# First batch of a fused attention and two MLPs: tile arithmetic and conversion steps set tile by tile

## The chip, the core and the metric

The kernel runs on one core of a Trainium2 chip. The metric is device time in microseconds (us). The engines are named as the profile names them: PE (TensorE, matmuls), DVE (VectorE), ACT (ScalarE), POOL (GpSimd) and SP (SyncE, which here only issues DMAs). Each engine runs its own instructions in order; so does each queue of DMA issues.

## The reference

```python
def _attn_ref(q, k, v, p):                       # batch 8, heads 8, seq 576, head_dim 64; p: 32 rows
    p_packed = sm_attn(p, k, v)
    return sm_attn(q, p_packed, p_packed)
def _moe_ref(x, w_in, w_out):                    # 4608 tokens, 512 -> 2048 -> 512
    h = x @ w_in
    g = h - np.tanh(h)
    return g @ w_out
def _moe2_ref(x, w_in, w_out, s, b):
    h = x @ w_in
    r = np.maximum(h, 0.0)
    return (s * (r * r) + b) @ w_out
```

The second MLP takes what the first returns, and the first takes the attention's output with the heads side by side. The weights of both MLPs come as 64-bit floats.

## The kernel before

Every product of the MLPs is made of three fp32r products of high and low parts: a value is rounded to fp32r (high), and the difference is the low part. The weights are first converted from 64-bit words to fp32 (`to_f32`, lines 113 to 130: one pass on ACT, line 119, then four on DVE, lines 121, 123, 126 and 129), and then, for the second layer, split (`split_seq`: the high part by ACT, line 138, the low part by DVE or POOL, line 140). First-layer weights come in four blocks of 512 columns, each converted in two halves of 1024 columns per partition (`w1_steps`); second-layer weights in 16 blocks of 512 (`wo1_steps`, blocks 0 to 15).

The tokens are worked on in 8 batches, each in two halves of 288 tokens. A tile is one block of 128 hidden units for one half: `mm1` (six matmuls, line 464), the tile arithmetic h - tanh(h) with its high and low parts, and, two or three tiles later, `mm2` (twelve matmuls, line 504). The first-layer weights are folded with the packed values of the batch (`make_z`), so that a tile needs z of its batch and the attention weights a2h and a2l of its half. A batch has 32 tiles; in the first batch they run as four parts of 8: first half with hidden blocks 0 to 7, second half with 0 to 7, first half with 8 to 15, second half with 8 to 15. Partial sums of the first two parts go to memory and come back (lines 522 and 527).

The tile arithmetic has three forms. "v": tanh on ACT, the subtraction on DVE (line 473), high part on ACT, low part on DVE (line 135). "b": the subtraction on DVE within the PSUM bank (line 481), high part by ACT, then PE subtracts the high part in the bank (line 487) and ACT copies the low part out (line 488). "p": as "b", but PE also subtracts the tanh (line 484), and DVE does nothing.

All other work is in two generators, from which steps are drawn: `fill` (conversion of the first MLP's weights, then the attention of the next batch: key scores `stage1`, z, `second_stage`) and `more` (conversion of the second MLP's weights, into memory). Six slots lie in each tile, one within mm1, one behind it, four within mm2. In the first batch, until second-layer block 15 is converted, each slot draws from `fill` by `SLOTS` (5, 3, 4 or 1 steps per six slots, by part) and each mm1 by `AFTER`; then, until the first half of batch 1 is through its attention, each mm1 draws four more. Within `first_weights` groups of generators run in turn, and the next group's first steps are drawn `AHEAD` of its turn. `until` draws steps by force where a tile needs what isn't done.

`FIRST_W` says at which steps of batch 0's own attention, before any tile, the first ten conversion steps (block 0 of the first layer) are drawn. The k, v and q of batches 1 to 7 are loaded through POOL's queue (lines 170, 177, 178 and 240), in pieces of 128 bytes for k and q; weights, partial sums and p through SP's.

## Time and profile before

| | us |
|---|---|
| median of 3 runs (1517.79 to 1522.28) | 1519.46 |
| the profiled execution | 1515.79 |
| its span | 1514.0 |
| PE busy | 1463.3 (97%) |
| DVE busy | 1074.3 (71%) |
| ACT busy | 754.1 (50%) |
| POOL busy | 357.9 (24%) |

The shares are means over a span of very different stages. The first batch is the first ninth of it, and it is there that PE's busy tenths fall below nine. So the page gives only the frame, and the rows further down are read from the trace within the first 172 us. Busy times of PE are modelled, since matmuls are pipelined: a busy share of PE in a short stretch is an upper end.

### The profile page before, as it was taken

The numbers are of one execution on the slowest core, as the hardware profiler recorded it, in microseconds if no ns is written. First come the engines' busy times: TensorE is split into PE (matmuls) and PEld (weight loads), VectorE is DVE, ScalarE is ACT, GpSimd is POOL, SyncE is SP. The second block draws the span as 40 slices with busy tenths as digits, with TensorE's granted clock in tenths as the row PEclk, the third lists the DMA queues.
The fourth block names the chain that finished last, engine by engine and source line by source line (L and its number), as shares of the span: only waits on it lengthen the run. The fifth ranks groups of instructions, "written<-read, shape, count | busy, mean of one in ns | idle before, by whom it ended". The sixth has DMA issues, their size and how long they took to land.

```text
span 1514.0 us, 28111 instructions
## 1 busy us (share of the span) xinstructions
PE 1463.3 (97%) x10508; PEld 1377.0 (91%) x10508; DVE 1074.3 (71%) x2058; ACT 754.1 (50%) x1459; POOL 357.9 (24%) x576
## 2 busy tenths in 40 slices
PE   6779899999999999999999999999999999999998
PEld 4668798998988889889999999999999999999998
DVE  5886878879687887875555767767777775565564
ACT  4554344444444344443344556656667655454443
POOL 0248452634447274543001000000021000000000
PEclk7899999999999999999999999999999999999999
DMA  9446355544535354332428466465487987676683
GB/s 283 162 135 169 105 147 138 155 132 120 150 98 151 92 141 118 103 94 95 147 100 308 178 229 235 172 260 214 194 296 284 312 258 199 217 239 200 216 248 84
DMA packets 252185, 271.62 MB, mean 179 GB/s; under 512 B 112784, under 2 KB 191888, under 8 KB 252048
## 3 DMA queue, kind: packets, MB, share of 16 engines
q1 hardware_dynamic: 225952, 222.68, 44.9%
q0 software_dynamic: 22368, 46.17, 11.4%
q8 instruction: 82, 1.34, 0.4%
q10 hardware_dynamic: 3728, 0.98, 0.3%
q14 instruction: 55, 0.45, 0.1%
HBM read 161.61 MB, written 108.13 MB: 178 GB/s over the span
## 4 chain that ended last, share of the span: by engine, by line
PE 79%; issue 7%; DVE 6%; DMA 3%; POOL 3%; ACT 2%; SPq 1%; DVEq 0%; POOLq 0%; ACTq 0%
PE acc L504 22%; PE h L464 11%; PE Y L1271 9%; PE Y L1045 8%; PE Z L1271 6%; PE X L1045 6%; PE Z L1045 6%; PE X L1271 6%; PE zp L367 2%; POOL k L170 1%; DMA k<-in_k_dram 1%; DVE gl L135 1%; PE pv L339 1%; SPq L194 1%; DMA g<-g 1%
## 5 line engine op out<-in xcount | busy, mean ns | idle before, releaser
L504 PE MATMUL acc<-gh,wo 128*128 128x288 f32 x2040 | 418.6, 296 | 0.2 <-DVE wo L140 0.2
L504 PEld LDWEIGHTS acc<-gh,wo 128*128 128x128 f32 x2040 | 329.8, 189 | 0.5 <-DVE wo L140 0.4
L504 PE MATMUL acc<-gl,wo 128*128 128x288 f32 x1020 | 309.8, 304 | 5.7 <-ACT wo L138 2.8
L472 ACT ACTIVATE t<-h 128x288 f32<-128x288 f32 x240 | 98.8, 412 | 304.4 <-PE h L464 263.5
L504 PEld LDWEIGHTS acc<-gl,wo 128*128 128x128 f32 x1020 | 192.4, 189 | 34.7 <-issue 20.0
L464 PE MATMUL h<-a2h,z 128*128 128x288 f32 x1024 | 213.9, 297 | 1.5 <-ACT z L445 1.5
L473 DVE TENSOR_TENSOR t<-h,t 128x288 f32<-128x288 f32 x240 | 107.5, 448 | 139.5 <-ACT t L472 138.8
L944 DVE TENSOR_TENSOR x<-B,x 128x768 fp32r<-128x768 f32 x158 | 147.0, 950 | 74.3 <-ACT x L1201 60.4
L464 PE MATMUL h<-a2l,z 128*128 128x288 f32 x512 | 157.9, 308 | 9.8 <-ACT gl L488 6.4
L464 PEld LDWEIGHTS h<-a2h,z 128*128 128x128 f32 x1024 | 165.0, 189 | 2.2 <-ACT z L445 1.7
L240 POOL DMA_DIRECT2D q<-in_q_dram x224 | 135.3, 612 | 130.7 <-DVE qT L374 109.3
L1045 PE MATMUL Y<-x,w 128*128 128x384 f32 x864 | 158.5, 336 | 0.0
L1271 PE MATMUL Y<-x,w 128*128 128x384 f32 x864 | 153.4, 335 | 0.0
L1045 PEld LDWEIGHTS Y<-x,w 128*128 128x128 f32 x864 | 151.3, 188 | 0.0
L1271 PEld LDWEIGHTS Y<-x,w 128*128 128x128 f32 x864 | 150.2, 188 | 0.5 <-ACT x L1201 0.3
L170 POOL DMA_DIRECT2D k<-in_k_dram x224 | 136.6, 617 | 50.2 <-DVE kT L290 40.7
L464 PEld LDWEIGHTS h<-a2l,z 128*128 128x128 f32 x512 | 97.4, 190 | 27.1 <-ACT gl L488 9.4
L1201 ACT CAST x<-B 128x768 fp32r<-128x768 f32 x116 | 93.8, 834 | 42.6 <-DMA B<-g 30.2
L135 DVE TENSOR_TENSOR gl<-t,gh 128x288 fp32r<-128x288 f32 x239 | 110.8, 463 | 0.0
L1045 PE MATMUL X<-x,w 128*128 128x384 f32 x576 | 108.1, 336 | 0.0
L1045 PE MATMUL Z<-x,w 128*128 128x384 f32 x576 | 107.9, 336 | 0.0
L1271 PE MATMUL X<-x,w 128*128 128x384 f32 x576 | 103.0, 336 | 1.5 <-DVE w L944 1.5
(181 smaller groups left out, 2236.4 us busy)
## 6 DMA issues: line engine op xcount, KB each, us to landing
g<-g SPq DMA_DIRECT2D x190, 384.0 KB, 3.3
B<-g SPq DMA_DIRECT2D x116, 384.0 KB, 4.7
w<-w_d POOLq DMA_DIRECT2D x28, 512.0 KB, 6.1
B<-x2t SPq DMA_DIRECT2D x24, 384.0 KB, 5.4
g<-s SPq DMA_DIRECT2D x23, 384.0 KB, 2.8
out_dram<-g SPq DMA_DIRECT2D x184, 48.0 KB, 1.9
x2t<-xs SPq DMA_DIRECT2D x15, 576.0 KB, 3.7
w1s<-in_moe_w_in_dram SPq DMA_DIRECT2D x16, 512.0 KB, 8.1
```

The costliest lines, as they stand in the source:

```text
L135: (eng or nc.vector).tensor_tensor(out=lo, in0=x, in1=hi.bitcast(F32), op=ALU.subtract)
L170: nc.gpsimd.dma_start(out=t[p0:p0 + 32, e], in_=rows[a][:, e, :, u * 32:u * 32 + 32])
L240: nc.gpsimd.dma_start(out=t[p0:p0 + 32], in_=src.rearrange("(n r) d -> r n d", r=32))
L367: nc.tensor.matmul(ps[e][i * M:(i + 1) * M, :rhs(i).shape[-1]], pblk[b][r, h // 4, h % 4 * M:h % 4 * M + M], rhs(i)[r], start=True, stop=True)
L464: nc.tensor.matmul(h[:, :HB], zt[:, zi, g, f0:f0 + P], a[:, g], start=(n == 0), stop=(n == 3 * G - 1))
L472: nc.scalar.activation(t, h[:, :HB], AF.Tanh)
L473: nc.vector.tensor_tensor(out=t, in0=h[:, :HB], in1=t, op=ALU.subtract)
L504: nc.tensor.matmul(acc[m][:, :HB], w[:, m * P:(m + 1) * P], x, start=(j == js[0] and i == 0), stop=(j == js[-1] and i == 2))
L944: self.nc.vector.tensor_tensor(out=o, in0=a, in1=b, op=op)
L1045: self.nc.tensor.matmul(bank[:, f, :self.TH], w[:, f, a, kt], x[:, b, kt], start=(p in ("P1", "P5", "P6") and m == 0), stop=(m == 5), skip ...
L1201: self.nc.scalar.copy(self.xs[(7 * self.NBK + n) % self.XS][:, 0], self.ready[0])
L1271: nc.tensor.matmul(bank[:, ft, :T], w[:, kk, u, ft], x[:, v, kk], start=first and p in ("P1", "P5", "P6"), stop=last, skip_group_check=True)
```

## The change

It sets, for the first batch, the form of the arithmetic of each of the 32 tiles (`HOW`: now 16 "p", 9 "b" and 7 "v") and the number of steps drawn in each tile's six slots (`STEPS`; these replace `SLOTS`, `AFTER` and `CATCH_UP`). It gives the low parts of blocks 2 to 11 to DVE, which POOL made. It issues the loads of batch 1's k, v and q on SP's queue instead of POOL's, and draws them ahead of the conversion of first-layer block 3 instead of behind it. Only conversions are drawn ahead of their turn, one step each. The first steps of the two halves of first-layer block 0 are drawn at steps 10 and 29 of the attention instead of 23 and 40, with the others moved too. `minus`, the negated identity, is made by POOL from zeros instead of by ACT.

```diff
-    AFTER, SLOTS = (6, 5, 4, 1), (5, 3, 4, 1)
-    HOW = "p" * 8, "b" * 8, "v" * 8, "v" * 8
-    AHEAD, CATCH_UP, FIRST_W = 13, 4, (23, 24, 25, 26, 27, 40, 41, 42, 43, 44)
+    STEPS = 9, 13, 14, 11, 15, 10, 12, 15, 0, 6, 9, 13, 7, 5, 0, 2, 6, 3, 10, 5, 6, 10, 11, 11, 18, 14, 15, 13, 12, 13, 10, 8
+    HOW = "ppbbpppppppppbvvvvvpppvvbbbpbbbp"
+    FIRST = (0, 0, 8), (1, 0, 8), (0, 8, 16), (1, 8, 16)
+    FIRST_W = 10, 15, 17, 25, 27, 29, 32, 40, 43, 44
...
-                        nc.gpsimd.dma_start(out=t[p0:p0 + 32, e], in_=rows[a][:, e, :, u * 32:u * 32 + 32])
+                        (nc.gpsimd if b > 1 else nc.sync).dma_start(out=t[p0:p0 + 32, e], in_=rows[a][:, e, :, u * 32:u * 32 + 32])
...
-            yield from split_wo(j, "wo1", nc.gpsimd if 1 < j < 12 else nc.vector, x)
+            yield from split_wo(j, "wo1", nc.vector, x)
...
-                    if i == min(AHEAD, 4 * len(group)) and n + 1 < len(groups):
-                        for g in groups[n + 1]:
-                            next(g)
+                    if i == len(group) and n + 1 < len(groups):
+                        for f, g in groups[n + 1]:
+                            if f in (w1_steps, wo1_steps):
+                                next(g)
...
-        nc.scalar.mul(minus, ident, -1.0)
+        nc.vector.memset(csum, 0.0)
+        nc.gpsimd.tensor_tensor(out=minus, in0=csum[:, 0], in1=ident, op=ALU.subtract)
...
+                [(second_loads,)],
                 [(w1_steps, 3, 0)], [(w1_steps, 3, 1)],
-                [(wo1_steps, 12), (wo1_steps, 13), (second_loads,)],
-                [(first_z, 3), (wo1_steps, 14), (wo1_steps, 15)])
+                [(first_z, 3), (wo1_steps, 12), (wo1_steps, 13)],
+                [(wo1_steps, 14), (wo1_steps, 15)])
...
-            if ("wo", NF - 1) not in done:
-                n = SLOTS[part[0]]
-                for _ in range(ticks[0] * n // 6 - (ticks[0] - 1) * n // 6):
+            if ("wo", NF - 1) in done and ticks[0] % 3 == 1:
+                next(more, None)
+            if ("a", 1, 0) in done or tile[0] >= len(STEPS):
+                next(fill, None)
+                return
+            n = STEPS[tile[0]]
+            for _ in range(ticks[0] * n // 6 - (ticks[0] - 1) * n // 6):
+                if ("a", 1, 0) not in done:
                     next(fill)
-                return
-            if ticks[0] % 3 == 1:
-                next(more, None)
-            next(fill, None)
...
-                    if ("wo", NF - 1) not in done:
-                        for _ in range(AFTER[part[0]]):
-                            next(fill)
-                    elif ("a", 1, 0) not in done:
-                        for _ in range(CATCH_UP):
-                            next(fill)
```

The order of instructions at three places, before and after. The changed file is three lines longer or shorter at places, so that line 121 of before is line 122 of after, and so on.

First place: DVE around the end of the conversion of second-layer blocks 10 and 11 (`t_10`, `t_11`, `wo1s_10`, `wo1s_11`; `wo1_10` and `wo1_11` hold the split blocks; `h_0_1_5` and `t_0_1_6` belong to tiles 13 and 14; `w1_3` is first-layer block 3). Before:

```order
L126 SCALAR_TENSOR_TENSOR t_10_933<-wo1s_10_761,t_10_933 128x512
L126 SCALAR_TENSOR_TENSOR t_11_935<-wo1s_11_763,t_11_935 128x512
L481 TENSOR_TENSOR h_0_1_3_964<-h_0_1_3_964,t_0_1_3_976 128x288
L129 SCALAR_TENSOR_TENSOR wo1s_10_761<-wo1s_10_761,t_10_933 128x512
L129 SCALAR_TENSOR_TENSOR wo1s_11_763<-wo1s_11_763,t_11_935 128x512
L481 TENSOR_TENSOR h_0_1_4_998<-h_0_1_4_998,t_0_1_4_1013 128x288
L121 TENSOR_SCALAR w1_3_836<-w1_3_836 128x1024
```

After:

```order
L130 SCALAR_TENSOR_TENSOR wo1s_10_758<-wo1s_10_758,t_10_920 128x512
L130 SCALAR_TENSOR_TENSOR wo1s_11_760<-wo1s_11_760,t_11_922 128x512
L141 TENSOR_TENSOR wo1_10_1010<-wo1s_10_758,wo1_10_1010 128x512
L141 TENSOR_TENSOR wo1_11_1012<-wo1s_11_760,wo1_11_1012 128x512
L482 TENSOR_TENSOR h_0_1_5_1034<-h_0_1_5_1034,t_0_1_5_1043 128x288
L474 TENSOR_TENSOR t_0_1_6_1093<-h_0_1_6_1086,t_0_1_6_1093 128x288
L474 TENSOR_TENSOR t_0_1_7_1117<-h_0_1_7_1110,t_0_1_7_1117 128x288
L136 TENSOR_TENSOR gl_1_0_1_7_1121<-t_0_1_6_1093,gh_1_0_1_7_1120 128x288
L122 TENSOR_SCALAR w1_3_862<-w1_3_862 128x1024
```

The two low parts now stand on DVE, and between them and block 3 only the arithmetic of tiles 13 to 15.

Second place: SP's queue from the load of second-layer block 13 (`wo1s`, 128x512) to that of blocks 14 and 15 (`wo1s`, 128x2x512); `x2t` and `xp` are partial sums. Before:

```order
L522 DMA x2t<-xs_0_906 512x1x288
L599 DMA wo1s_1033<-in_moe_w_out_dram 128x512
L229 DMA pc_1085<-in_p_dram 128x2x64 x2
L581 DMA wo1s_1088<-in_moe_w_out_dram 128x2x512
L522 DMA x2t<-xs_1_1273 512x1x288
```

After:

```order
L600 DMA wo1s_1038<-in_moe_w_out_dram 128x512
L230 DMA pc_1061<-in_p_dram 128x2x64 x2
L171 DMA k_0_0_1067<-in_k_dram 32x9x32 x8
L171 DMA k_0_1_1076<-in_k_dram 32x9x32 x8
L178 DMA v_0_1125<-in_v_dram 64x4x320
L179 DMA v_0_1125<-in_v_dram 64x4x256
L241 DMA q_0_0_0_1137<-in_q_dram 32x9x32 x4
L241 DMA q_0_0_1_1142<-in_q_dram 32x9x32 x4
L241 DMA q_0_1_0_1147<-in_q_dram 32x9x32 x4
L241 DMA q_0_1_1_1152<-in_q_dram 32x9x32 x4
L582 DMA wo1s_1229<-in_moe_w_out_dram 128x2x512
```

Thirty-four loads of batch 1 now stand ahead of blocks 14 and 15.

Third place: ACT around its first pass over second-layer block 14 (`t_14`); `t_0_0_8` is the tanh of tile 16, `t_0_0_10` that of tile 18, `t_0_0_11` that of tile 19. Before:

```order
L138 CAST wo1_13_1179<-wo1s_13_1033 128x512
L488 CAST gl_0_1_6_1112<-h_0_1_6_1072 128x288
L119 ACTIVATE t_14_1200<-wo1s_7_1088 128x512
L485 CAST gh_0_1_7_1167<-h_0_1_7_1135 128x288
L119 ACTIVATE t_15_1217<-wo1s_7_1088 128x512
L432 CAST z_0_3_1189<-zp_0_3_0_1190 128x512
L472 ACTIVATE t_0_0_8_1220<-h_0_0_8_1208 128x288
```

After:

```order
L473 ACTIVATE t_0_0_10_1259<-h_0_0_10_1250 128x288
L135 CAST gh_1_0_0_10_1262<-t_0_0_9_1204 128x288
L120 ACTIVATE t_14_1266<-wo1s_7_1229 128x512
L433 CAST z_0_3_1231<-zp_0_3_0_1232 128x512
L433 CAST z_0_3_1231<-zp_0_3_1_1233 128x512
L480 ACTIVATE t_0_0_11_1295<-h_0_0_11_1287 128x288
L136 CAST gh_1_0_0_11_1299<-t_0_0_10_1259 128x288
```

The pass stands two to three tiles later, right behind tile 18's tanh and ahead of tile 19's.

## Rows read from the trace of the kernel before

**Rows 1.** Busy time by stretch: stretch, length, PE, PEld, DVE, ACT, POOL, clock, DMA.

```profile
36.00:94.90 58.90, 46.79 (x284) 37.14 (x284) 52.03 (x91) 34.67 (x74) 10.76 (x8) 0.89 0.45 164
94.90:171.60 76.70, 65.65 (x578) 52.64 (x576) 57.54 (x132) 36.25 (x96) 55.85 (x88) 1.00 0.58 143
...
111.40:171.60 60.20, 54.78 (x497) 44.01 (x497) 42.97 (x110) 26.84 (x75) 42.51 (x71) 1.00 0.59 145
171.60:262.00 90.40, 88.56 (x794) 80.21 (x788) 73.78 (x194) 43.04 (x114) 41.28 (x68) 1.00 0.49 130
```

**Rows 2.** PE's timeline: start, duration; the first matmuls of tiles 16 and 32.

```profile
111.38 0.40 PE L464 MATMUL h<-a2l,z 128*128 128x288 f32 x1 [1.49 <-ACT gl L488]
...
171.62 0.40 PE L464 MATMUL h<-a2l,z 128*128 128x288 f32 x1
```

**Rows 3.** DVE's groups by line and shape, 14 to 260 us: busy us, mean ns | idle.

```profile
L473 DVE TENSOR_TENSOR t<-h,t 128x288 f32<-128x288 f32 x48 | 21.5, 448 | 25.3 <-ACT t L472 25.2
L135 DVE TENSOR_TENSOR gl<-t,gh 128x288 fp32r<-128x288 f32 x47 | 21.0, 446 | 0.0
L126 DVE SCALAR_TENSOR_TENSOR t<-wo1s,t 128x512 int32<-128x512 int32 x15 | 10.9, 754 | 0.0
...
L123 DVE TENSOR_SCALAR t<-t 128x512 int32<-128x512 int32 x16 | 8.0, 536 | 0.0
L121 DVE TENSOR_SCALAR t<-t 128x512 f32<-128x512 f32 x16 | 7.5, 498 | 2.7 <-ACT t L119 2.5
...
L126 DVE SCALAR_TENSOR_TENSOR cv<-w2s,cv 128x512 int32<-128x512 int32 x6 | 4.1, 684 | 0.1
...
L481 DVE TENSOR_TENSOR h<-h,t 128x288 f32<-128x288 f32 x8 | 3.7, 458 | 3.1 <-ACT t L479 3.1
...
L140 DVE TENSOR_TENSOR wo<-wo1s,wo 128x512 fp32r<-128x512 f32 x5 | 3.2, 682 | 0.1
...
L123 DVE TENSOR_SCALAR cv<-cv 128x512 int32<-128x512 int32 x6 | 2.5, 419 | 0.0
L121 DVE TENSOR_SCALAR cv<-cv 128x512 f32<-128x512 f32 x6 | 2.5, 413 | 0.0
```

**Rows 4.** DVE's timeline: start, duration, instruction, idle time before it.

```profile
27.18 0.85 DVE L389 STREAM_TRANSPOSE t<-s 128x288 f32<-128x288 f32 x2 [0.29 <-PE s L367]
...
93.63 1.28 DVE L129 SCALAR_TENSOR_TENSOR wo1s<-wo1s,t 128x512 int32<-128x512 int32 x2
...
97.73 1.69 DVE L123 TENSOR_SCALAR w<-w 128x1024 int32<-128x1024 int32 x1
...
102.94 0.69 DVE L123 TENSOR_SCALAR w<-w 128x1024 int32<-128x1024 int32 x1
...
136.25 1.10 DVE L290 STREAM_TRANSPOSE kT<-k 128x288 f32<-128x288 f32 x2 [1.35 <-DMA k<-in_k_dram]
...
166.79 0.83 DVE L418 TENSOR_TENSOR a2l<-a,a2h 128x288 fp32r<-128x288 f32 x2 [0.95 <-ACT a2h L416]
```

**Rows 5.** POOL's timeline, its last low parts and its first loads of batch 1.

```profile
95.82 3.04 POOL L140 TENSOR_TENSOR wo<-wo1s,wo 128x512 fp32r<-128x512 f32 x2 [4.97 <-ACT wo L138]
98.81 6.77 POOL L170 DMA_DIRECT2D k<-in_k_dram  x10
```

**Rows 6.** PE's timeline in a "p" tile: the subtraction of the tanh, and the next matmul.

```profile
66.54 0.65 PE L484 MATMUL h<-t,minus 128*128 128x288 f32 x2
66.81 0.51 PE L464 MATMUL h<-a2l,z 128*128 128x288 f32 x1
```

**Rows 7.** ACT's groups by line and shape, 36 to 172 us.

```profile
L488 ACT CAST gl<-h 128x288 fp32r<-128x288 f32 x16 | 6.4, 398 | 3.7 <-PE h L487 3.7
```

**Rows 8.** SP's timeline: DMA issues, with their count.

```profile
99.28 0.94 SPq L229 DMA_DIRECT2D pc<-in_p_dram  x2
...
1429.28 3.92 SPq L1233 DMA_DIRECT2D out_dram<-g  x8
```

**Rows 9.** DMA issues, 98 to 140 us: count, size, median us to landing.

```profile
wo1s<-in_moe_w_out_dram SPq DMA_DIRECT2D x1, 1024.0 KB, 8.3
```

More of the change, by code (lines that the diff above doesn't have):

```diff
@@ L176, in load_v @@
         src = v[b, 4 * g:4 * g + 4].rearrange("h (r c) d -> r h (c d)", c=C)
-        nc.gpsimd.dma_start(out=t[:R], in_=src[:, :, :CT * D])
-        nc.gpsimd.dma_start(out=t[R:, :, :(C - CT) * D], in_=src[:, :, CT * D:])
+        (nc.gpsimd if b > 1 else nc.sync).dma_start(out=t[:R], in_=src[:, :, :CT * D])
+        (nc.gpsimd if b > 1 else nc.sync).dma_start(out=t[R:, :, :(C - CT) * D], in_=src[:, :, CT * D:])
         v_t[b, g] = t.rearrange("r h (c d) -> r h c d", c=CT)
@@ L239, in load_q @@
                         p0 = (2 * e + u) * 32
-                        nc.gpsimd.dma_start(out=t[p0:p0 + 32], in_=src.rearrange("(n r) d -> r n d", r=32))
+                        (nc.gpsimd if b > 1 else nc.sync).dma_start(out=t[p0:p0 + 32], in_=src.rearrange("(n r) d -> r n d", r=32))
                 q_t[b, hf, g, hp] = t
@@ L639, in in_turn @@
         def in_turn(*groups):
-            groups = [[call_late(g) for g in group] for group in groups]
+            groups = [[(f, f(*a)) for f, *a in group] for group in groups]
             for n, group in enumerate(groups):
-                for i, _ in enumerate(both(group)):
+                for i, _ in enumerate(both([g for _, g in group])):
                     yield
-                    if i == min(AHEAD, 4 * len(group)) and n + 1 < len(groups):
-                        for g in groups[n + 1]:
-                            next(g)
-        def call_late(f):
-            g, *a = f
-            yield from g(*a)
+                    if i == len(group) and n + 1 < len(groups):
+                        for f, g in groups[n + 1]:
+                            if f in (w1_steps, wo1_steps):
+                                next(g)
         def until(key, gen):
@@ L814, in slot @@
                 next(fill, None)
-            if ("wo", NF - 1) not in done:
-                n = SLOTS[part[0]]
-                for _ in range(ticks[0] * n // 6 - (ticks[0] - 1) * n // 6):
+            if ("wo", NF - 1) in done and ticks[0] % 3 == 1:
[6 more added lines that the diff above has]
+                if ("a", 1, 0) not in done:
                     next(fill)
-                return
-            if ticks[0] % 3 == 1:
-                next(more, None)
-            next(fill, None)
+        tile = [-1]
         owed = [0]
@@ L834, in pack_attention_two_mlps @@
             else:
-                parts = [(hf, js) for js in (range(NF // 2), range(NF // 2, NF)) for hf in range(2)]
+                parts = [(hf, range(j0, j1)) for hf, j0, j1 in FIRST]
             for hf, js in parts:
@@ L848, in pack_attention_two_mlps @@
                     c = j // CH
+                    tile[0] += 1
                     until(("z", b, c), fill)
@@ L851, in pack_attention_two_mlps @@
                     h = mm1(b, hf, j, slot)
-                    if ("wo", NF - 1) not in done:
-                        for _ in range(AFTER[part[0]]):
-                            next(fill)
-                    elif ("a", 1, 0) not in done:
-                        for _ in range(CATCH_UP):
-                            next(fill)
                     if j % CH == CH - 1:
                         mm1_done.add((b, hf, c))
-                    how = HOW[part[0]][j - js[0]] if b == 0 else "v"
+                    how = HOW[tile[0]] if b == 0 else "v"
                     on_pe = how != "v"
```

## The prediction

> **What bounds the kernel now.** I read the table by stretches first. From 171.6 us on, the second batch takes 90.4 us for its 32 tiles with TensorE (PE) busy for 88.56 us: PE is the bound there, and 90.4 / 32 = 2.83 us is what a tile costs with all that belongs to it [rows 1]. The first batch is another matter: its 32 tiles need 36.0 to 171.6 us, 135.6 us, and PE waits. Tile numbers below count from 0 in program order; tile 32, the first of the second batch, starts at 171.62 us [rows 2]. Nothing in the diff touches what comes after it, so the whole effect is the shift of that one moment.
>
> Inside the first batch I split at 94.9 us, where VectorE (DVE) ends the last conversion step of second-layer block 11 (93.63 + 1.28) [rows 4]. Before that point DVE is busy for 52.03 of 58.9 us, 88%: it is the bound. After it DVE has 57.54 in 76.7 us, 75%, and nothing is full [rows 1]. So before 94.9 us the change is priced by DVE's work; behind it by how closely DVE and PE can be packed.
>
> **The change, part by part.** *Tile arithmetic (HOW).* Before: 8 tiles "p" (nothing on DVE), 8 "b" (one subtraction), 16 "v" (two). After: 16, 9, 7. A "v" costs DVE 21.5/48 + 21.0/47 = 0.895 us, a "b" 3.7/8 = 0.46 us [rows 3]. Before 16 x 0.895 + 8 x 0.46 = 18.0, after 7 x 0.895 + 9 x 0.46 = 10.4: -7.6 us. Of this -0.9 lies ahead of 94.9 us (two "b" more in tiles 2 and 3, four "b" fewer in tiles 8 to 11) and -6.7 behind it. PE and ScalarE (ACT) take it over: 8 passes with the fp32 tanh, after each of which the next matmul starts 0.27 us later [rows 6], and 9 more subtractions of gh, taken at the same 0.27 as an upper end: 4.6 us on PE; 9 x 0.40 = 3.6 us on ACT [rows 7]. Both have that much idle time in this batch.
>
> *Low parts of blocks 2 to 11 on DVE instead of POOL.* 10 x 3.2/5 = +6.4 us of DVE [rows 3]. Against it: while POOL runs such a subtraction, DVE instructions stretch. The step at 97.73 us took 1.69 us beside POOL's pair at 95.82, the same step at 102.94 us 0.69 [rows 4, 5]. Over all, the 512-wide steps of the first batch against the same steps on the second MLP's weights, which have no such neighbour: 16 x (0.498 - 0.413) + 16 x (0.536 - 0.419) + 15 x (0.754 - 0.684) = 4.3 us [rows 3], and with the 1.0 us of the one wide step 5.3. That the stretch goes away with POOL's work is the better reading of these rows; the other end is 0. I take -5.3, all but 1.0 of it ahead of 94.9 us. Also, block 11 was ready only when POOL ended, 95.82 + 3.04 = 98.86 us [rows 5].
>
> *Steps by tile (STEPS), no catching up.* The same conversions, emitted elsewhere: behind block 11's split stand only four tile subtractions until tile 16, and the eight wide steps of first-layer block 3 follow that tile instead of preceding it (order, first place). Five steps on the second MLP's weights stand before tile 32 where nine stood. The four that go, three of 128 columns and one of 896, are an estimate of 1280 x 0.684/512 = 1.7 us [rows 3], moved into the second batch, where PE is the bound and DVE has 90.4 - 73.8 = 16.6 us idle [rows 1]: free. If that cover were gone they would cost their 1.7 us.
>
> *Loads of batch 1 by SP.* POOL issues ten in 6.77 us [rows 5]; for SP the nearest row is a store in pieces of 128 bytes, eight in 3.92 us, 0.49 us each [rows 8]. POOL's time is off the path. But SP's queue runs in order, and now 16 + 2 + 16 of these loads stand between the load of block 13 and that of blocks 14 and 15 (order, second place). This is the one place where the change adds a wait; it is the first rival. The last k transposes waited 1.35 us for their load [rows 4]. The Trainium skill, "SBUF — State Buffer", in its box on the "DVE blocks DMA" trap, says that a DVE instruction in a two-port mode keeps POOL from writing its descriptors, and that issuing from SP avoids it; by that rule the 1.35 us would go, and the sum below would read 1.35 us less. The trace shows POOL's ten loads without a gap, so I take 0.
>
> *Two conversions begun sooner in the attention.* DVE reaches the score transposes at 27.18 us having waited 0.29 us for PE [rows 4]: the conversions are not what holds it, and starting them sooner gains nothing. Ends: a gain of 0.3, and a loss if ACT's two wide passes, which now stand among the exponentials, come too early; at 0.398 us for 288 columns [rows 7] a 1024-wide pass is an estimate of 1.4 us, so at most 2.8. Taken: 0. Building "minus" on POOL: 0, it is read long after.
>
> **The sum.** Block 11 ready: 94.9 + 6.4 - 0.9 - 4.3 = 96.1 us. Three tiles with next to nothing on DVE (tile 13 to 16) at 2.83: tile 16 starts at 104.6. DVE work left to tile 32: 57.5 - 6.7 - 1.0 - 1.7 - 1.8 (the four subtractions) = 46.3 us. At what share? Before, from tile 16 at 111.4 us on it was 43.0 of 60.2, 71%, in the second batch 73.8 of 90.4, 82% [rows 1, 2]. Both limits are near each other here: 16 tiles x 2.83 = 45 us on PE and some 4 us of new subtractions. I take the middle, 76%: 60.9 us. Tile 32 starts at 165.5, which is 6.1 us sooner. The ends: 82% gives 161.1 (-10.5), 71% gives 169.8 (-1.8). The profiled execution took 1515.79 us (span 1514.0), so it would be 1509.7; the median of the runs shown is 1519.46, 3.7 above it, and the same shift puts the median at 1513.4.
>
> **Rivals.** *1. SP's queue gives the gain back.* Block 13's load can go when block 11 is done, 96.1; then 0.94 for p, as before, and 34 x 0.49 = 16.7 [rows 8]: blocks 14 and 15 are issued at 114 and land 8.3 us later [rows 9], 122. ACT meets its first pass over them right behind tile 18's tanh (order, third place), 104.6 + 2 x 2.83, about 110. It would stand for up to 12 us, and behind it in its queue stand two casts of z, tile 19's tanh and gh for tile 18; PE runs dry two tiles on. Some of this is hidden: DVE has about 5 us of queued steps, and the bound is its work. Of the 46 us some 9 lie ahead of this point (the eight wide steps at twice the 512-wide ones, and a few tile subtractions); 37 / 0.76 = 49 us behind 122 gives 171, no gain: 1519. For it: the row of 8.3 us and the order. Against: the 5 us that DVE does meanwhile take the result half-way back. 0.24.
> *2. Tight packing.* The stand is short and the share 82%: 10.5 us or more, 1508. For it: PE at 98% in the second batch by the same program text. Against: there one step is emitted per slot, here about two, so that each hop of the attention has less time. 0.18.
> *3. Slower: the second half of batch 1's keys.* Their 16 loads stand behind rival 1's weights in SP's queue and behind the store and load of partial sums, and wait for the first half's transposes. If blocks 14 and 15 land at 122, their DVE steps and the first four transposes (an estimate of 7 us from the 512-wide rows) end at about 131; 16 x 0.49 = 7.8 more is 139, and a landing, between 0 and the 8.3 us of the larger load, puts the last transposes at 139 to 147, say 143. Before, they began at 136.25, and from there to tile 32 took 35.4 us, with the last step of the softmax at 166.79 [rows 2, 4]. If that chain keeps its length, tile 32 starts at 178.4, 6.8 later: 1526. It decides as soon as these transposes begin past 141, with the chain as long as before. Against it: 10 steps a tile were emitted there, now about 13. 0.11.
> *4. No difference* for other reasons, say all steps forced at the same places: 1519. 0.05.
>
> **How the numbers follow.** The forecast, 1513.4, has 0.42. About 0.3% (4.6 us) is what a measurement of this kernel can tell from no change. Of the forecast's own spread, 1509.0 to 1517.7, about two thirds lie below 1514.9, so faster has 0.18 + 0.29, and 0.08 from rival 1 when it is half hidden: 0.55. Slower, past 1524.0, has what of rival 3 lies there, 0.10, and the same the rest, 0.35. The range, with about one in ten left out at either end, is 1506 to 1522.
>
> **What would show it.** In the profile after: no POOL subtraction in the first batch and 512-wide DVE steps all near 0.42 and 0.68; block 11's split ending near 96; tile 16 starting near 104 to 105 instead of 111.4; ACT's pass over blocks 14 and 15 with an idle time "until DMA wo1s" (rival 1, over 5 us); the last k transposes of batch 1 near 139 (rival 3 past 141); tile 32 near 165; and from there to the end the same 1342 us as before. I am wrong if tile 16 doesn't come sooner, or if the gain at tile 16 is gone at tile 32.

## The result

The changed kernel takes 1527.12 us (median of 10 runs, 1523.01 to 1530.53), the kernel before 1518.33 in as many runs beside it (1515.83 to 1522.28). The ratio is 1.0056 with a 95% interval from 1.0046 to 1.0067: slower by 8.5 us. The prediction was 1513.4, faster, with a range up to 1522. The profiled execution took 1529.15 us with a span of 1527.4; the one before took 1515.79. So the two profiles that are compared here differ by 13.4 us, more than the medians do.

The first step in reading it is to write down when the same tiles start in both traces (first matmul of the tile, us from the start; the last column is after minus before):

| tile | before | after | difference |
|---|---|---|---|
| 0 | 35.7 | 33.8 | -1.9 |
| 13 | 96.9 | 88.6 | -8.3 |
| 16 | 111.4 | 96.6 | -14.8 |
| 18 | 116.4 | 108.3 | -8.1 |
| 20 | 122.8 | 119.1 | -3.7 |
| 32 | 171.6 | 165.1 | -6.5 |
| 34 | 174.9 | 171.0 | -3.9 |
| 40 | 192.0 | 187.7 | -4.3 |
| 136 | 465.5 | 462.8 | -2.7 |
| 148 | 503.0 | 505.5 | +2.5 |
| 173 | 573.4 | 583.4 | +10.0 |
| 206 | 668.6 | 683.0 | +14.4 |
| 248 | 781.1 | 793.9 | +12.8 |

So the first batch does end sooner, nearly as forecast: tile 32 starts at 165.1, and the prediction said 165.5. The loss comes 300 us later, in three jumps, from tile 140 to 148, from 148 to 173 and from 200 to 206, where the diff changes no line.

**The first batch after.** The windows that answer to [rows 1] (stretch, length, PE, PEld, DVE, ACT, POOL, clock, DMA):

```profile
36.00:88.60 52.60, 44.78 (x290) 36.91 (x290) 50.97 (x97) 34.91 (x76) 0.00 (x0) 0.92 0.48 182
...
96.60:165.10 68.50, 60.29 (x518) 49.42 (x517) 47.00 (x107) 33.05 (x88) 11.09 (x18) 0.93 0.62 132
165.10:258.40 93.30, 91.62 (x806) 81.12 (x805) 74.64 (x196) 44.46 (x117) 41.20 (x68) 1.00 0.49 131
```

Up to tile 13 DVE is now busy for 50.97 of 52.6 us, 97%, where it had 88%. From tile 16 to tile 32 it has 47.00 of 68.5, 69%. In the second batch, which ends at 258.4, PE is as full as before, 91.62 of 93.3 us; its 32 tiles take 2.9 us longer, nearly all of it in the first two (see "Tile 32 as a gauge" below).

DVE's groups by shape, 14 to 260 us, against [rows 3] (busy us, mean ns, idle before):

```profile
L141 DVE TENSOR_TENSOR wo<-wo1s,wo 128x512 fp32r<-128x512 f32 x15 | 9.8, 688 | 1.5 <-ACT wo L139 1.0
...
L127 DVE SCALAR_TENSOR_TENSOR t<-wo1s,t 128x512 int32<-128x512 int32 x15 | 9.7, 682 | 0.0
...
L122 DVE TENSOR_SCALAR t<-t 128x512 f32<-128x512 f32 x16 | 6.1, 420 | 0.3 <-ACT t L120 0.3
L124 DVE TENSOR_SCALAR t<-t 128x512 int32<-128x512 int32 x16 | 6.1, 418 | 0.0
```

The stretch beside POOL's subtractions is gone, as the prediction read it: 498, 536 and 754 ns have become 420, 418 and 682.

PE's timeline at tiles 16, 18 and 32 (start, duration, idle time before), against [rows 2]:

```profile
96.58 0.29 PE L465 MATMUL h<-a2l,z 128*128 128x288 f32 x1
...
102.11 1.06 PE L368 MATMUL zp<-w,pblk 64*32 64x512 f32 x8 [0.57 <-DVE w L130]
106.48 1.93 PE L368 MATMUL zp<-w,pblk 64*32 64x512 f32 x8 [3.30 <-DVE w L130]
108.34 0.61 PE L465 MATMUL h<-a2l,z 128*128 128x288 f32 x1
...
165.11 0.51 PE L465 MATMUL h<-a2l,z 128*128 128x288 f32 x1
```

Behind tile 17 stand the products of z for first-layer block 3, which wait for the eight wide steps. In the kernel before these products, a single run of 16, waited for nothing:

```profile
108.81 1.09 PE L367 MATMUL zp<-w,pblk 64*32 64x512 f32 x16
```

The granted clock of PE, which is 1.00 from 94.9 to 171.6 us in the kernel before [rows 1], falls twice in the changed one, in a wait of 3.30 us ahead of tile 18 and again at 119.0 us, a microsecond behind a wait of 2.91 us for ACT:

```profile
105.30:112.20 6.90, 5.72 (x24) 4.06 (x25) 4.10 (x10) 0.73 (x2) 0.00 (x0) 0.51 0.49 73
119.00:122.40 3.40, 2.94 (x12) 2.50 (x12) 3.04 (x7) 2.67 (x6) 0.00 (x0) 0.50 1.05 271
```

Tile 18's first matmul takes 0.61 us there, tile 16's took 0.29. At half the clock half of PE's busy time is lost: an estimate of 2.9 us in the first stretch and 1.5 in the second. The prediction had no term for it.

And rival 1's wait is there. SP's queue ahead of blocks 14 and 15, against [rows 8]:

```profile
90.41 8.20 SPq L171 DMA_DIRECT2D k<-in_k_dram  x16
...
100.04 9.45 SPq L241 DMA_DIRECT2D q<-in_q_dram  x16
109.59 0.40 SPq L582 DMA_DIRECT2D wo1s<-in_moe_w_out_dram  x1
```

ACT's timeline, the first pass over block 14:

```profile
116.02 0.66 ACT L120 ACTIVATE t<-wo1s 128x512 f32<-128x512 f32 x1 [5.10 <-DMA wo1s<-in_moe_w_out_dram]
```

SP takes 0.51 us for a k load and 0.59 for a q load, where the prediction took 0.49; the load of blocks 14 and 15 goes out at 109.59 and ACT stands for 5.1 us.

**The loss.** The view of waits, 262 to 835 us, has one wait of DVE for POOL's column sums before (us in total, times, longest):

```profile
DVE cv L752 <- POOL csum L744: 5.5, 1, 5.5
```

and after:

```profile
DVE cv L752 <- POOL csum L744: 21.2, 4, 6.2
...
PE cs L768 <- POOL csum L744: 4.5, 1, 4.5
```

`csum` is a sum over the columns of the second MLP's output weights, taken while they are converted (`more`): per unit POOL makes two additions (line 744), and DVE's step of line 752 overwrites what they read. POOL also issues the k and q loads of the next batch. Its timeline at the second jump, in the kernel before:

```profile
542.19 9.66 POOL L240 DMA_DIRECT2D q<-in_q_dram  x16
555.58 1.65 POOL L744 TENSOR_TENSOR csum<-csum,cv 128x256 f32<-128x256 f32 x2 [3.73 <-DVE cv L129]
558.07 8.45 POOL L170 DMA_DIRECT2D k<-in_k_dram  x14 [0.83 <-DVE kT L290]
```

and in the changed one:

```profile
554.79 9.64 POOL L241 DMA_DIRECT2D q<-in_q_dram  x16
...
566.40 8.41 POOL L171 DMA_DIRECT2D k<-in_k_dram  x14 [0.28 <-DMA q<-in_q_dram]
574.83 1.65 POOL L744 TENSOR_TENSOR csum<-csum,cv 128x256 f32<-128x256 f32 x2
```

DVE's there, in the changed kernel:

```profile
575.60 0.29 DVE L752 TENSOR_TENSOR cv<-cv 128x128 f32<-128x128 f32 x1 [5.43 <-POOL csum L744]
```

PE's:

```profile
576.53 1.02 PE L768 MATMUL cs<-ones,csum 128*128 128x2 f32 x4 [4.50 <-POOL csum L744]
```

The sums need 1.65 us, but stand behind 8.41 us of k loads in POOL's queue, and these behind 16 q loads; before, they stood between the two. DVE waits 5.43 us for them, with the next tiles' arithmetic queued behind it. PE stands for 4.50 us: here its own product of the sums (`cs`, line 768) is next in its queue. Then the second half of the price, in the windows around that moment:

```profile
571.20:576.40 5.20, 0.82 (x7) 0.58 (x5) 0.81 (x3) 0.73 (x2) 5.11 (x9) 1.00 0.26 57
```

```profile
576.40:583.20 6.80, 6.67 (x28) 6.66 (x29) 3.08 (x10) 1.49 (x4) 1.50 (x4) 0.50 0.96 216
```

PE is busy for 0.82 of 5.2 us, and the granted clock then is 0.50, the lower of its two levels (1.2 GHz), for 6.8 us of full work: about half of that, 3.4 us, is lost on top of the 4.5 us of idle time. Together that is 7.9 us, and the step in the table between tiles 148 and 173 is 7.5. The clock fell at the other two jumps as well:

```profile
501.30:504.70 3.40, 3.40 (x20) 1.74 (x21) 1.78 (x5) 1.07 (x2) 0.00 (x0) 0.50 1.06 266
675.40:682.20 6.80, 6.07 (x26) 6.07 (x27) 4.43 (x13) 1.73 (x5) 1.30 (x3) 0.50 0.93 206
```

Before, it stayed at 1.00 from 86.6 us nearly to the end.

### The profile page after: what moved, and what is told of

The parts are those of the page before. It is cut to its first block, busy times and chain, and to the rows that moved or that the text cites. A ratio compares the mean times of both kernels' runs of the same rounds, so it can differ in the third digit from the quotient of the medians.

```text
span 1527.4 us, 28158 instructions
## 1 busy us (share of the span) xinstructions
PE 1476.8 (97%) x10533; PEld 1389.2 (91%) x10533; DVE 1062.4 (70%) x2052; ACT 758.5 (50%) x1467; POOL 302.7 (20%) x499
## 5 line engine op out<-in xcount | busy, mean ns | idle before, releaser
L505 PE MATMUL acc<-gh,wo 128*128 128x288 f32 x2040 | 423.4, 299 | 0.2 <-DVE wo L141 0.2
L505 PEld LDWEIGHTS acc<-gh,wo 128*128 128x128 f32 x2040 | 334.3, 191 | 0.5 <-DVE wo L141 0.4
L473 ACT ACTIVATE t<-h 128x288 f32<-128x288 f32 x231 | 95.0, 411 | 311.2 <-PE h L465 271.4
L474 DVE TENSOR_TENSOR t<-h,t 128x288 f32<-128x288 f32 x231 | 103.6, 448 | 145.8 <-ACT t L473 144.3
L171 POOL DMA_DIRECT2D k<-in_k_dram x192 | 116.5, 614 | 186.9 <-DVE kT L291 166.1
L241 POOL DMA_DIRECT2D q<-in_q_dram x192 | 116.0, 612 | 122.4 <-DVE qT L375 106.5
L136 DVE TENSOR_TENSOR gl<-t,gh 128x288 fp32r<-128x288 f32 x230 | 104.7, 455 | 3.8 <-ACT gh L135 3.8
```

The source lines that it names most:

```text
L136: (eng or nc.vector).tensor_tensor(out=lo, in0=x, in1=hi.bitcast(F32), op=ALU.subtract)
L171: (nc.gpsimd if b > 1 else nc.sync).dma_start(out=t[p0:p0 + 32, e], in_=rows[a][:, e, :, u * 32:u * 32 + 32])
L241: (nc.gpsimd if b > 1 else nc.sync).dma_start(out=t[p0:p0 + 32], in_=src.rearrange("(n r) d -> r n d", r=32))
L473: nc.scalar.activation(t, h[:, :HB], AF.Tanh)
L474: nc.vector.tensor_tensor(out=t, in0=h[:, :HB], in1=t, op=ALU.subtract)
L505: nc.tensor.matmul(acc[m][:, :HB], w[:, m * P:(m + 1) * P], x, start=(j == js[0] and i == 0), stop=(j == js[-1] and i == 2))
```

## Experiment 1: is it the order of sums and loads on POOL?

The theory: `more`, which makes the sums, and `fill`, which issues the loads, are drawn side by side, and the change shifts one against the other by some five steps. `LAND` is the number of steps that `more` lets pass before its first conversion, so it moves the sums against the loads and leaves `fill` as it is. In the order on POOL from batch 2 on, 8 in the changed kernel gives the kernel before's sequence of sums and loads again, and 19 in the kernel before gives the changed kernel's. In the sequence of before, the 16 q and the 16 k loads stand in a row ahead of a pair of sums once; in the changed kernel's they do so three times, and three of DVE's four waits are there. The rival is that the loss belongs to the work in the first batch or to traffic. One other thing moves with `LAND`: with 8, nine of `more`'s steps on DVE stand before tile 32 again, as in the kernel before, and not five.

The changed kernel with the old sequence:

```diff
-    LAND = 14
+    LAND = 8
```

> The changed kernel with the second MLP's weight conversions begun 6 steps sooner (LAND 8 instead of 14), which puts POOL's sums of output weights back where they stood among the loads before the change. Theory (the loss is DVE waiting for POOL's csum, which stands behind 16 loads in POOL's queue; 21.2 us of such waits after, 5.5 before): the waits fall to about 5.5 us, tile 32 stays near 165 us, and the time is 1510 to 1516 us, faster than before. Rival (the loss comes from batch 1's loads on SP or from the new tile forms, and the csum waits only stand in for it): tile 32 near 165, but still 1524 to 1530 us.

Measured 1518.66 us (1516.77 to 1520.28), ratio to the kernel before 0.9999 [0.9987, 1.0011]. The loss is gone; a gain does not show, where 1510 to 1516 was expected. In the two profiles the lead is 4.3 us at tile 32 and 2.3 at tile 136, then 0.0 at tile 140, behind the one wait that the kernel before has too:

```profile
DVE cv L752 <- POOL csum L744: 6.3, 1, 6.3
```

PE around it (tile 139 and the step behind it), in the kernel before and here:

```profile
474.95 0.40 PE L464 MATMUL h<-a2l,z 128*128 128x288 f32 x1 [1.39 <-DVE t L473]
...
476.79 0.90 PE L339 MATMUL pv<-v,e1T 128*32 128x64 f32 x40 [1.18 <-ACT e1T L98]
```

```profile
473.51 0.40 PE L465 MATMUL h<-a2l,z 128*128 128x288 f32 x1 [2.22 <-DVE t L474]
...
475.35 1.05 PE L340 MATMUL pv<-v,e1T 128*32 128x64 f32 x40 [1.18 <-ACT e1T L99]
```

and the window behind that:

```profile
475.80:479.30 3.50, 3.50 (x36) 3.21 (x25) 2.29 (x9) 0.73 (x2) 1.26 (x2) 0.51 0.80 231
```

PE stood for 2.22 us where it stood for 1.39 before, and this time the clock fell to the lower level. With a wait that is 0.8 us longer and 3.5 us at half the clock, the whole lead of 2.3 us was gone.

The kernel before with the changed kernel's sequence:

```diff
-    LAND = 14
+    LAND = 19
```

> The kernel before with the second MLP's weight conversions begun 5 steps later (LAND 19 instead of 14), which gives POOL's queue the changed kernel's order of sums and loads and nothing else of the change. Theory: csum waits of about 21 us instead of 5.5, 1529 to 1536 us. Rival: 1516 to 1521 us as before.

Measured 1540.73 (1536.38 to 1542.68, 4 runs), ratio 1.0143 [1.0111, 1.0174], above the expected 1529 to 1536. The waits, 262 to 835 us:

```profile
DVE cv L752 <- POOL csum L744: 20.3, 5, 6.3
...
PE cs L768 <- POOL csum L744: 6.8, 1, 6.8
```

The kernel before alone, with its first batch hardly moved (tile 40 at 190.3), loses 22 us by the sequence. So the loss is not the first batch's doing. Why the same order costs this kernel more than the changed one is open; in its profile PE stands for more than 1 us six times between 440 and 700 us, the longest time for 6.79.

## Experiment 2: the sums on VectorE

If the sums are the cause, they cost little where no load stands ahead of them. The same edit in both kernels:

```diff
-                        nc.gpsimd.memset(csum, 0.0)
+                        nc.vector.memset(csum, 0.0)
...
-                        nc.gpsimd.tensor_tensor(out=csum, in0=csum, in1=xa[:, 2 * kh:2 * kh + 2], op=ALU.add)
+                        nc.vector.tensor_tensor(out=csum, in0=csum, in1=xa[:, 2 * kh:2 * kh + 2], op=ALU.add)
```

> The changed kernel with the sums of the output weights (and their zeroing) made by DVE instead of POOL, so that they stand behind no loads. Theory: no csum wait at all, at a price of 32 DVE adds of about 0.4 us in batches 4 to 6, where PE is the bound: 1505 to 1514 us. Rival (the loss is elsewhere): 1524 to 1532 us.

> The kernel before with the sums of the output weights made by DVE. Theory: its one csum wait of 5.5 us goes, 32 adds come in: 1512 to 1518 us; the difference to the changed kernel with the same edit is then the first batch alone, 3 to 7 us. Rival: no change, 1518.

The changed kernel: 1511.21 (1510.2 to 1513.8), ratio 0.9958 [0.9945, 0.9971]. The kernel before: 1513.86 (1513.28 to 1517.21), ratio 0.9978 [0.9962, 0.9994]. DVE's group of the sums in the changed one:

```profile
L744 DVE TENSOR_TENSOR csum<-csum,cv 128x256 f32<-128x256 f32 x32 | 13.5, 423 | 0.8
```

In the changed kernel PE stood three times for more than 1 us between 440 and 700 us, for 2.21, 4.50 and 3.03; with the sums on DVE it does so not once, and from 123 us nearly to the end the granted clock stays at 1.00. 13.5 us more on DVE, where it has room, remove 0.0098 of the changed kernel's time, 15 us, and 0.0022 of the other's, 3.3 us. With the sums out of the way the change is worth 0.0020, some 3 us, with intervals that overlap; the medians differ by 2.65. This is what the prediction had at 6.1.

Is anything left of the shift without the sums? The changed kernel with both edits (sums by `nc.vector`, `LAND = 8`):

> The changed kernel with the column sums on VectorE and the loads let through 8 steps after their signal instead of 14, so that the steps of the second MLP stand to the loads as before the change. Theory: with the sums off POOL the phase no longer costs the 18 us, but a small rest of it stays: between tiles 40 and 200 the run with the sums on VectorE and 14 gave back some 2.4 us against the kernel before with the same edit (it led by 3.7 us at tile 40, by 1.3 at tile 200), and the run with 8 gave back 0.2 up to tile 136. So this run should keep the lead of tile 40 and come out at 1508 to 1510. Rival: with no sums on POOL the phase is worth nothing, and the run equals the one with 14, 1511 within 1.

(`LAND` counts steps of `more`, not of the loads, as said above.) Measured 1511.18 (1510.64 to 1511.65), ratio 0.9939 [0.9922, 0.9955], against 1511.21 and 0.9958 with 14. The medians are the same, and the theory's 1508 to 1510 was missed; by the ratios this run is 2.9 us faster, with intervals that overlap. So without sums on POOL the shift costs some 3 us or less by these runs, and that it costs anything is not shown. Nearly its whole price is the sums in that queue.

## Experiment 3: the parts of the change

Each of these starts from the changed kernel with the sums on VectorE (ratio 0.9958) and undoes one part. They ran beside runs of the kernel before of their own, so the ratios compare best: 0.0010 is 1.5 us. Each ratio has an interval of some 0.0013 to either side, 2 us, so a difference of two of them below about 3 us is not clear of the noise.

Forms of the tile arithmetic:

```diff
-    HOW = "ppbbpppppppppbvvvvvpppvvbbbpbbbp"
+    HOW = "p" * 8 + "b" * 8 + "v" * 16
```

> The changed kernel with the column sums on VectorE and the tile arithmetic of before (8 p, 8 b, 16 v); everything else as changed. It puts 6.7 us of DVE work back behind 88.6 us and takes 4.6 us off PE. Theory A, the sum of the prediction: DVE's work sets the first batch, so tile 32 starts 6 to 9 us later than 165.9 and the time is 1517 to 1520. Theory B: behind 96 us DVE is busy for 69 per cent only, and three waits set the batch (z behind first-layer block 3, ACT behind the load of blocks 14 and 15, the attention of batch 1); the forms then cost 0 to 3 us, 1511 to 1514.

Measured 1517.88 (1514.54 to 1520.24), ratio 0.9985 [0.9973, 0.9998]: the new forms gain 4.1 us by the ratios, 6.7 by the medians. Theory A's size fits the medians. Of the 6.7 us that it puts back on DVE, the window from tile 16 to tile 32 shows half, 50.41 us of DVE for 46.97 in the run with the sums on VectorE:

```profile
102.00:172.90 70.90, 60.68 (x498) 48.58 (x498) 50.41 (x119) 29.13 (x78) 11.08 (x18) 0.90 0.61 127
```

Low parts of blocks 2 to 11:

```diff
-            yield from split_wo(j, "wo1", nc.vector, x)
+            yield from split_wo(j, "wo1", nc.gpsimd if 1 < j < 12 else nc.vector, x)
```

> The changed kernel with the column sums on VectorE and the low parts of blocks 2 to 11 made by POOL again. By the prediction's terms DVE loses 6.4 us of work and gets 5.3 us of stretch back, and block 11 is ready later by POOL's last pair (some 4 us). Theory: these nearly cancel up to 88.6 us (DVE is busy for 97 per cent there), tile 16 starts 0 to 4 us later, and the waits behind it hide most of that: 1511 to 1513. Rival: POOL's stretch is smaller than 5.3 us and DVE gains, 1507 to 1510.

Measured 1516.3 (1514.41 to 1516.63), ratio 0.9973 [0.996, 0.9985]: DVE's making them gains 2.3 us by the ratios, whose intervals overlap, and 5 by the medians. DVE's groups show the stretch again:

```profile
L122 DVE TENSOR_SCALAR t<-t 128x512 f32<-128x512 f32 x16 | 8.2, 547 | 0.6 <-ACT t L120 0.5
```

and POOL's timeline what is ready late, blocks 8 to 11 in one run that ends at 95.13 us:

```profile
86.62 8.51 POOL L141 TENSOR_TENSOR wo<-wo1s,wo 128x512 fp32r<-128x512 f32 x4 [16.99 <-ACT wo L139]
```

Tile 16 starts at 100.4 instead of 97.2. So the two terms do not quite cancel; that POOL's end decides is a reading of this row, not tested by itself. The median is 3.3 us above the expected range.

Loads of batch 1 on POOL again (four places like this one):

```diff
-(nc.gpsimd if b > 1 else nc.sync).dma_start(
+(nc.gpsimd if b > 0 else nc.sync).dma_start(
```

> The changed kernel with the column sums on VectorE and the loads of batch 1 on POOL's queue again. The load of blocks 14 and 15 then stands behind two small loads on SP instead of 34 more and is issued some 17 us sooner, so ACT's wait of 5.1 to 5.5 us for it goes away. Theory A: that wait is on the path of the first batch, and tile 32 starts 3 to 5 us sooner: 1506 to 1508.5. Theory B: z behind block 3 and the attention of batch 1 hide it: 1510 to 1512. Slower than 1512 would mean that issuing on SP had itself a worth.

Measured 1509.16 (1508.22 to 1511.77), ratio 0.9927 [0.9912, 0.9943]: faster by 4.7 us by the ratios, 2 by the medians, and between the ranges of the two theories. SP issues blocks 14 and 15 right behind block 13:

```profile
96.31 0.41 SPq L582 DMA_DIRECT2D wo1s<-in_moe_w_out_dram  x1
```

ACT's wait is gone, and between tiles 18 and 20 the kernel gains 3.7 us. So rival 1's mechanism cost the change 2 to 5 us. This is the fastest kernel of the study.

The edit does a second thing. POOL has no low parts to make any more, so nothing stands ahead of these loads in its queue, and they go out some 90 us sooner, beside the prelude's own loads:

```profile
1.88 9.22 POOL L171 DMA_DIRECT2D k<-in_k_dram  x15
```

SP's five v loads of the prelude take 12.29 us to issue, where they took 8.77 with the loads on SP, and tile 0 starts at 39.4. In the four profiles with these loads on POOL's empty queue it starts at 39.3 to 39.5, in the eleven others at 33.8 to 37.0. So this kernel pays 2 us or more in its prelude, and what the shorter queue on SP gives behind it is larger than the total shows: from tile 0 to the end this profile takes 1470.6 us, that with the loads on SP 1474.9. A kernel that holds the loads back until the prelude is over was not run.

The ten first steps at their old places:

```diff
-    FIRST_W = 10, 15, 17, 25, 27, 29, 32, 40, 43, 44
+    FIRST_W = 23, 24, 25, 26, 27, 40, 41, 42, 43, 44
```

> The changed kernel with the column sums on VectorE and the ten first conversion steps drawn at the old steps of batch 0's attention. The prediction took this edit at 0, between a gain of 0.3 and a loss of 2.8 us. In the profiles so far tile 0 starts at 33.8 to 39.4 us with the new steps and at 35.7 to 37.0 with the old ones, and the new ones differ among themselves by TensorE's clock. Theory: no gain to be seen, 1510 to 1512.5. Rival: the 2 us by which the profile of the changed kernel began earlier are the edit's, so this run takes 1513 to 1514.

Measured 1513.11 (1511.41 to 1513.9), ratio 0.9954 [0.9942, 0.9967]: no difference by the ratios. The median is 0.6 above the theory's range and just within the rival's, in company with that of the kernel before, 1520.29 in these runs and 1518.56 beside the first. Tile 0 starts at 35.9 here, and at 33.8 to 36.8 with the new steps where no load stands in the way: the 1.9 us at tile 0 in the first table are not shown to be the edit's.

All three parts undone together, so that the schedule and the prelude are left:

> The changed kernel with the column sums on VectorE and three parts undone together: forms of the arithmetic as before, low parts of blocks 2 to 11 on POOL, loads of batch 1 on POOL. What is left of the change is the schedule (STEPS and the order of the groups) and the steps of the prelude. Theory A, the parts add up: 6.3 for the forms and 4.7 for the low parts are lost, 2.5 won with the loads, so 1519 to 1521; the schedule alone then costs 5 to 7 us against the kernel before with the sums on VectorE (1513.9). Theory B, the two gains overlap (both free DVE): 1514 to 1517, and the schedule costs little.

Measured 1515.9 (1512.58 to 1517.27), ratio 0.9969 [0.9958, 0.998]. In us this lies in theory B's range, but theory A's was built on differences of medians. By the ratios the three parts make 4.1 + 2.3 - 4.7 = 1.7 us, and 0.9969 against 0.9958 is 1.7. So the parts may well add up, though all this is within the noise, and with POOL's low parts ahead of them the loads go out at 97.05 here and not in the prelude. The schedule alone cannot be told from the kernel before with the sums on VectorE (0.9978).

## Experiment 4: the stand behind tile 17

Of the 14.8 us of lead at tile 16, 11.1 are gone at tile 20. SP's loads and the lower clock are a part of it; the products of z are in the way too. The order shows how that came: the change draws z of block 3 (`first_z`, 3) together with blocks 12 and 13, right behind block 3's conversion, where the kernel before drew it with 14 and 15. All three runs start from the fastest kernel (sums on VectorE, loads on POOL). In that one PE waits in front of tile 18:

```profile
107.96 1.06 PE L368 MATMUL zp<-w,pblk 64*32 64x512 f32 x8 [0.57 <-DVE w L130]
...
112.33 1.93 PE L368 MATMUL zp<-w,pblk 64*32 64x512 f32 x8 [3.31 <-DVE w L130]
```

First more steps in tiles 13 to 16, where DVE stands idle:

```diff
-    STEPS = ..., 7, 5, 0, 2, 6, 3, 10, 5, ...
+    STEPS = ..., 7, 7, 6, 6, 5, 5, 7, 5, ...
```

> The changed kernel with the column sums on VectorE, the loads of batch 1 on POOL's queue, and more steps drawn in tiles 13 to 16 (7, 6, 6, 5, 5, 7 instead of 5, 0, 2, 6, 3, 10 in tiles 13 to 18), so that first-layer block 3 is converted while tiles 14 to 16 run. In the run with the loads on POOL DVE stands idle for 1.2, 2.4 and 2.1 us in tiles 13 to 15, then works off the eight wide steps without a pause, and tile 18 starts 9.4 us after tile 17, where a tile takes 2.4 to 2.8 elsewhere. Theory A: that stand is the schedule's and on the path; tile 18 comes 4 to 6 us sooner and the time is 1503 to 1506. Theory B: the attention of batch 1 and the transposes of its keys set the end of the batch, and they absorb it: 1508 to 1510.

Measured 1515.15 (1513.55 to 1516.13), ratio 0.997 [0.9957, 0.9982]: slower by 6 us, against both theories. PE's waits came along, now in front of tile 16:

```profile
102.50 1.06 PE L368 MATMUL zp<-w,pblk 64*32 64x512 f32 x8 [1.36 <-DVE w L130]
...
106.86 1.93 PE L368 MATMUL zp<-w,pblk 64*32 64x512 f32 x8 [3.30 <-DVE w L130]
```

Then z drawn later, alone, and with the steps:

```diff
-                [(first_z, 3), (wo1_steps, 12), (wo1_steps, 13)],
-                [(wo1_steps, 14), (wo1_steps, 15)])
+                [(wo1_steps, 12), (wo1_steps, 13)],
+                [(first_z, 3), (wo1_steps, 14), (wo1_steps, 15)])
```

> The run with the column sums on VectorE and the loads of batch 1 on POOL, and z of first-layer block 3 drawn together with blocks 14 and 15, as before the change, instead of with blocks 12 and 13. In the changed kernel the products of this z stand on PE ahead of tile 18 and wait 0.6 and 3.3 us for the two halves of block 3, though no tile before tile 20 reads this z. With more steps in tiles 13 to 16 the same two waits came ahead of tile 16. Here they stand behind tile 19's first matmuls. Theory A: PE's queue, stopped at these products, is what costs; tile 18 then starts 3 to 5 us sooner than in the run with the loads on POOL, and the time is 1504.5 to 1507 against its 1509.2. Theory B: DVE's steps, not the place of z, set this stretch; tile 20 and the end stay where they were, 1508 to 1511.

> As the run before it, and more steps drawn in tiles 13 to 16 (7, 6, 6, 5, 5, 7 in tiles 13 to 18). The products of z of block 3 then stand ahead of tile 18, some 8 DVE steps behind the end of block 3's conversion, and should not wait. Theory A: with both, PE does not wait in tiles 16 to 20, so tile 20 starts 3 to 6 us sooner than with the loads on POOL alone, and if the loss in tiles 25 to 32 seen with the steps alone (6 us) was due to that stand, the time is 1503 to 1506. Theory B: that loss has its own cause in the attention of batch 1 and stays, so 1509 to 1514.

Measured 1515.4 (1514.44 to 1518.25), ratio 0.9969 [0.9955, 0.9983], and 1512.79 (1510.82 to 1513.36), ratio 0.9944 [0.9929, 0.9958]. Neither beats 0.9927, and the first is outside the ranges of both its theories. The second is within theory B's. Tile 18 does start sooner with z alone moved, at 106.7 instead of 114.2, but tile 20 starts at 122.1 instead of 121.9. PE's timeline there:

```profile
109.52 0.37 PE L505 MATMUL acc<-gl,wo 128*128 128x288 f32 x1 [1.85 <-DVE gl L136]
...
112.52 0.61 PE L505 MATMUL acc<-gl,wo 128*128 128x288 f32 x1 [2.37 <-DVE xs L101]
```

and with the steps too:

```profile
106.20 0.40 PE L505 MATMUL acc<-gl,wo 128*128 128x288 f32 x1 [2.58 <-DVE gl L136]
...
115.61 0.40 PE L505 MATMUL acc<-gl,wo 128*128 128x288 f32 x1 [1.18 <-DVE xs L101]
```

Tile 0 starts at 39.3 to 39.5 in these four profiles and tile 20 at 121.9, 122.1, 122.1 and 120.2: whichever wait is taken away, another comes up, for the tile arithmetic or the partial sums that now stand behind the conversions in DVE's queue. Theory A falls. That DVE's work in the stretch sets it is not shown: it is busy for 18 to 23 of the 27.7 us from 94.3 to 122.0, PE for 22 to 24, and PE's granted clock is 0.88 in three of the four and 0.94 in the last. All three orders then lose 5 to 6 us against the fastest kernel between tiles 25 and 32, in the attention of batch 1. Why is open.

## Why the prediction was wrong

**The step that failed** is the sentence that nothing in the diff touches what comes after tile 32, with its twin in the part on the schedule: four steps on the second MLP's weights move into the second batch, and that is free. On DVE no price of it shows. But the steps of `more` are also the ones that POOL's sums stand among, and drawn later they meet the load bursts at other places. The prediction checked the moved steps on the engine that executes them and not on the queues that the generator's later steps share with `fill`. Tile 32 to the end was to take 1342 us as before; it took 1527.4 - 165.1 = 1362.3, with 21.2 us of DVE's waits for the sums where there were 5.5, and with three stretches at the lower clock between 501 and 683 us where there was none. The order on POOL's queue, which is read without a run, has this in it, as experiments 1 and 2 show from both sides.

**Tile 16 and what follows.** The prediction put block 11's end at 96.1 and tile 16 at 104.6; they came at 89.0 and 96.6. The terms were right in size (688 ns for a low part, a stretch of 4.2 us gone by the groups above). Wrong was to carry DVE's idle time along: 6.9 us of it lay ahead of 94.9 us [rows 1], and 1.6 are left. Another 1.9 us stand at tile 0 already. Idle time of an engine at 88% was slack that the new order could take up, not a constant. Behind tile 16 the same error has the other sign: a share of 76% was taken between 71 and 82, and it is 69, with waits at z and at blocks 14 and 15 and the lower clock. The two errors cancel at tile 32, so the hit there, 165.1 for 165.5, is luck.

**Tile 32 as a gauge.** 6.5 us sooner there, but 3.9 at tile 34. In the kernel before a run of 16 products of z stands directly ahead of tile 32; in the changed one it stands behind tile 33:

```profile
170.01 1.68 PE L367 MATMUL zp<-w,pblk 64*32 64x512 f32 x16 [2.48 <-DVE z L435]
```

```profile
168.31 1.09 PE L368 MATMUL zp<-w,pblk 64*32 64x512 f32 x16
```

The start of a single matmul is a fair gauge only if the same work lies behind it. The first batch's gain is about 4 us in these two profiles, 1.9 of it at tile 0, and some 3 by experiment 2, not 6.1.

**The rivals.** Rival 1 was the right mechanism: issue at 109.6 instead of the 114 of its working, a stand of 5.1 us instead of up to 12, a price of 2 to 5 us by the run with the loads on POOL, which pays for its early loads besides. Rival 2's packing did not come. Rival 3 did not happen: the last key transposes begin at 137.62, below the 141 from which it decides. The slower end that came was none of the listed ones.

**Small terms.** The prelude was taken at 0, and no difference shows. The wait of 1.35 us of the last key transposes [rows 4] is gone; but it is also gone with the loads on POOL, where these transposes begin at 139.12 without a wait. So this case does not bear out that the rule of the Trainium skill, "SBUF — State Buffer", on the "DVE blocks DMA" trap explains that wait; the later moment of the transposes would explain it as well.

## What to carry to other kernels

When an edit changes how many steps of a background stream run before some point, its phase against every other stream changes for the rest of the program. Print the order of each in-order queue to the end, for the engines that the edit does not name above all, and look where short work with a reader stands behind a burst of DMA issues. Better, give such work to a queue without bursts: here that was worth 15 us in the changed kernel and 3 in the kernel before, as much as the change itself, and with the loads of batch 1 back on POOL it gave 1509.16 us, 0.9927 of the kernel before.

## What the runs showed of the hardware

- Sums of 1.65 us stood behind 14 loads of 36 KB that took POOL 8.41 us to issue, 0.60 us each: on POOL a DMA issue occupies the queue like an instruction. Such a sum is two additions; one takes 423 ns on DVE.
- A stand of PE cost more than its length here. 4.5 us of waiting were followed by 6.8 us at the lower clock with PE busy for 6.67. Idle times of 1.39 and 1.18 us in a row left the clock up in the kernel before; 2.22 and 1.18 at the same place were followed by the lower level in experiment 1.
- One and the same prelude varies by some 3 us, and its clock with it. The changed kernel and the run with `LAND` 8 differ in nothing ahead of tile 0. The 16 products of z in the first, where the mean granted clock from 14.0 to 33.8 us is 0.82, and in the second, where it is 0.61:

```profile
27.38 1.45 PE L368 MATMUL zp<-w,pblk 64*32 64x512 f32 x16 [0.57 <-DVE t L390]
```

```profile
28.60 2.32 PE L368 MATMUL zp<-w,pblk 64*32 64x512 f32 x16 [0.57 <-DVE t L390]
```

Tile 0 starts at 33.8 in the first and at 36.6 in the second. A difference of 2 us at tile 0 between two profiles says nothing about an edit.
- Loads that are issued early can cost where they land among others: with 34 loads of batch 1 going out from 1.88 us on, five v loads took SP 12.29 us instead of 8.77, and tile 0 started at 39.3 to 39.5 in all four profiles of that kind.
